# Two empty steps in the chain that scales an attention block by its softmax sums, and another split of the row-max tiles between two stages

## The chip, the cores and the metric

The kernel runs on one core of a Trainium2 chip. The metric is device time in microseconds (us), measured over whole executions; lower is better. Beside the times there is one profiled execution, whose trace tells what each engine did: TensorE (PE, with its weight loads as PEld), VectorE (DVE), ScalarE (ACT), GpSimd (POOL) and SyncE (SP), which here only issues DMAs. Every engine takes its instructions in the order in which the program wrote them.

## The reference

One input x of 2048 tokens by 640 channels goes through two branches that a gate mixes:

```python
g = sigmoid((x * gate_w).sum(-1, keepdims=True))
# a: attention, 32 query heads of 20 channels, one shared key and value head
q = (x @ wq), k = x @ wk, v = x @ wv
p = softmax(q k^T * 20 ** -0.5);  a = (p @ v) @ wo
# b: token-mixing MLP, along the tokens: 2048 -> 1728 -> 2048
h = layernorm(x);  u = gelu(h^T w1 + b1);  b = (u w2 + b2)^T
out = g * a + (1 - g) * b
```

All data are 32-bit floats. Products that need it are made from a high and a low part of each operand (three matmuls for one).

## The kernel before, in words

**Attention.** A unit n (0 to 31) is one block of 512 queries for a group of four heads; it has sixteen key blocks of 128 keys. For each key block PE makes four score tiles (L703, operands K=62 rows, in two row halves of the array), ScalarE takes their exponentials (L712), and `pv_group` (L728) multiplies them with v for all four heads into one bank (sixteen L738 matmuls for two key blocks). A column of ones behind v gives the softmax sums in the same bank, one row for each head. ScalarE copies the bank out (L747, L750) and POOL adds the copies up in `acc` (L751).

The exponent needs the maximum of each row beforehand. For that PE makes the scores of every unit a second time, as *max tiles* (L491), 32 for each row half and unit, 2048 in all, and VectorE reduces each to a column (L497). After 64 tiles VectorE takes the final maximum (L512), POOL negates and splits it (L514 to L516), and VectorE turns it (L523); the result goes through DRAM (m_scr) into two rows of the q tile (L531).

**The chain of a unit's sums.** When a unit's last key blocks are added up, `pv_group` puts a list of steps into `later`. In the loop these are: `sums_out` (L773, four rows of sums to l_scr in DRAM), `sums_in` (L776, back as 128x16 into `rl`), `inverse` (L780, VectorE's reciprocal, and its DMA to l_scr, L781), `inverse_in` (L785, four broadcast reloads into `ot`), `scale` (L789, POOL multiplies acc by ot), `high` (L792, POOL) and `low` (L795, POOL, and eight stores to o_scr, L799). The output product reads o_scr. In the tail (`keep`) the chain is another one, all on VectorE and POOL.

**Stretches.** `main(k, ...)` (L1096) writes one stretch of the order: score tiles, max tiles and 15 to 24 steps of another product, dealt to the two row halves by a pattern of letters and a small model of when PSUM banks come free, and at its end the PV group of two key blocks. There are 244 stretches (`ph`): 84 with the first MLP product (L1004), 128 with the second (L816), 32 with the output product of the first eight row tiles (L949). A unit lasts eight of them. `settle()` (L1060) is called in the middle of a stretch and at its end; each call takes one step from `later` (two once all max tiles are done, `spare`) and one from the gelu chain. So a chain of seven steps lasts three and a half stretches. At the end of a stretch the order is: `ms_done` (the final maximum), `settle`, `fetch_max`, the `rest` of the stretch (loads and splits of weights on SP and POOL, L105 to L130), `store_max`, and then the PV group.

**Shares of max tiles.** `share(k)` (L1079) says how many max tiles each half gets in stretch k. `base` holds what the pattern has. Up to `m` (the end of the first MLP product) a stretch gets its pattern, less one in every fourth; from `m` on, the tiles that are left are dealt in proportion to the patterns that are left:

```python
        if k >= m:
            return [(x * c[k] + sum(c[k:]) // 2) // sum(c[k:]) for x, c in zip(left, base)]
```

**Tail.** After the stretches come 13 blocks with the last 26 key blocks, the output products of the other row tiles (L904, added up by VectorE, L912) and late loads from o_scr (L879); before them the program asserts that `later` is empty.

Of the kernel before, what the change touches and what calls it, by code (L numbers as in the profile page):

```python
# [32 lines left out]
NA = 8  # L33
# [7 lines left out]
def mix_kernel(ctx: ExitStack, tc: tile.TileContext, A_x, A_wq, A_wk, A_wv, A_wo,  # L41
# [5 lines left out]
    def f32(ap):  # L47
        return ap.bitcast(F32)
# [123 lines left out]
    with tc.tile_pool(name="pa", bufs=1) as pa, \  # L172
# [114 lines left out]
        def transpose_x(sb, cs):  # L287
            pts = [(pst if c < 4 else psa).tile([P, NB], F32, name="pt" if c < 4 else "pp") for c in cs]
            for i in range(4):
                for c, pt in zip(cs, pts):  # L290
                    nc.tensor.transpose(pt[:, i * P:(i + 1) * P], xts[4 * sb + i][:, c * P:(c + 1) * P], ident)
            return [(sb, c, pt) for c, pt in zip(cs, pts)]
# [102 lines left out]
        for sb in range(NQB):  # L395
# [11 lines left out]
            for m in range(DC):  # L407
                turned = []
                if sb + 1 < NQB and m > 1 and (sb, m) != (2, DC - 1):
                    turned = transpose_x(sb + 1, ((0, 1), (2, 3), (4,))[m - 2])  # L410
# [46 lines left out]
    def bank_take():  # L457
        i = min(range(len(pool)), key=lambda j: pool[j][0])
        return pool.pop(i)[1]
# [8 lines left out]
    def busy(engine, us):  # L468
        clock[engine] = max(clock[engine], clock["now"]) + us
# [256 lines left out]
    later = []  # L726

    def pv_group(us, keep=False):  # L728
        n, kb = units[us[0]]
        assert units[us[-1]][0] == n  # L730
        if not otile:
            otile.append(bank_take())
        o = otile[0]
        opened = not keep or kb == 0 or us[0] == len(units) - TAIL
        ends = kb + len(us) == NS
        for i, u in enumerate(us):
            for hh in range(4):
                nc.tensor.matmul(o[32 * hh:32 * hh + 32, :], v_sb[:, kb + i, :], ptiles.pop((u, hh)),  # L738
                                 start=opened and i == 0, stop=(i == len(us) - 1) and (ends or not keep),
                                 skip_group_check=True)  # L740
        if not keep:
            begin = max(clock["act"], clock["pv"] + 0.14)
            clock["act"] = begin + 0.477
            pool.append((begin + 0.65, otile.pop()))
            if kb == 0:
                sums[0] = ev.tile([P, NB], F32, name="acc", bufs=2)
                nc.scalar.activation(sums[0], o, AF.Copy)  # L747
            else:
                part = ev.tile([P, NB], F32, name="part", bufs=2)
                nc.scalar.activation(part, o, AF.Copy)  # L750
                nc.gpsimd.tensor_add(sums[0], sums[0], part)  # L751
        if ends and n < NU - 1:
            qb, g = divmod(n, NQ)
            ot = ev.tile([P, NB // 32, 32], F32, name="ot")
            rl = ev.tile([P, NB // 32], F32, name="rl")
            on = sums[0]
            flat = ot.rearrange("p c e -> p (c e)")
            oh, ol = flat.bitcast(F32R), on.bitcast(F32R)
            if keep:
                nc.vector.tensor_add(on, on, o)  # L760

            def turned():
                nc.vector.transpose(flat, on)
                nc.vector.reciprocal(rl, ot[:, :, DH])
                nc.vector.tensor_mul(ot, ot, rl[:, :, None].to_broadcast([P, NB // 32, 32]))

            def back():
                nc.vector.transpose(on, flat)

            def sums_out():  # L770
                for hh in range(4):
                    r = 32 * hh + DH
                    nc.sync.dma_start(out=l_scr[0, n, hh:hh + 1], in_=on[r:r + 1, :])  # L773

            def sums_in():
                nc.sync.dma_start(out=rl, in_=l_scr[0, n].rearrange("h (r c) -> (h r) c", r=32))  # L776

            def inverse():
                busy("dve", 0.17)
                nc.vector.reciprocal(rl, rl)  # L780
                nc.sync.dma_start(out=l_scr[1, n].rearrange("h (r c) -> (h r) c", r=32), in_=rl)  # L781

            def inverse_in():
                for hh in range(4):
                    nc.sync.dma_start(out=flat[32 * hh:32 * hh + 32, :],  # L785
                                      in_=l_scr[1, n, hh:hh + 1].to_broadcast([32, NB]))

            def scale():
                nc.gpsimd.tensor_mul(on, on, flat)  # L789

            def high():
                nc.gpsimd.tensor_copy(oh, on)  # L792

            def low():
                nc.gpsimd.tensor_sub(ol, on, f32(oh))  # L795
                for j, t in enumerate((oh, ol)):
                    for hh in range(4):
                        r = (4 * g + hh) * DH
                        nc.sync.dma_start(out=o_scr[j, r:r + DH, qb * NB:(qb + 1) * NB],  # L799
                                          in_=f32(t[32 * hh:32 * hh + DH, :]))  # L800

            first = (None, turned, back) if keep else (sums_out, sums_in, inverse, inverse_in, scale)
            later.extend((False, f) for f in (*first, high, low))

    def b2_jobs(st):
# [226 lines left out]
    def stretches(seq):  # L1032
        return [(rows[1 - b], rest if b else [], done if b else []) for rows, rest, done in seq for b in range(2)]

    ph = stretches(seq)
    m = len(ph)
# [37 lines left out]
    def pattern(k):  # L1074
        return PATTERN[len(ph[k][0]) if visits[k] else 0]

    base = [[pattern(k)[int(k % 2 != h)].count("m") for k in range(len(ph))] for h in range(2)]

    def share(k):  # L1079
        left = [32 * NU - x for x in given]  # L1080
        if k >= m:
            return [(x * c[k] + sum(c[k:]) // 2) // sum(c[k:]) for x, c in zip(left, base)]
        over = [sum(c[k:]) - x for x, c in zip(left, base)]
        h = over.index(max(over))
        return [c[k] - (i == h and k % 4 == 1 and over[h] > 0) for i, c in enumerate(base)]

    lanes = [0.0, 0.0]
    fresh = [True, True]
# [7 lines left out]
    def main(k, vs, n_max):  # L1096
# [65 lines left out]
        if vs:  # L1162
            start = max([max(lanes) + DRAIN, min(e for e, _ in pool)] + [ready[v] for v in vs])
            clock["pv"] = start + len(vs) * PV_US + ENTER
            lanes[:] = [clock["pv"]] * 2
            fresh[:] = [True, True]
            pv_group(vs)
# [7 lines left out]
    for k in range(len(ph)):  # L1175
        n = visits[k]
        main(k, list(range(v, v + n)), share(k))
        v += n
        if k == len(ph) - 4:
            raw = last_wo()  # L1180
        if k == len(ph) - 2:
            w_last = split_last(raw)
# [4 lines left out]

    pool.append((lanes[0], ps_g.tile([P, NB], F32, name="g")))
    begin = lanes[0]
    assert not later  # L1190
    otile.append(bank_take())
    for i in range(4):
        tail_load(NS - 4 - NA + i, late=True)
# [1 line left out]
    for n in BLOCKS:  # L1195
# [25 lines left out]
        for _ in range(n):  # L1221
            settle()
            pv_group([v], True)
            v += 1
# [88 lines left out]
```

## Time and profile before

| | us |
|---|---|
| median of 3 runs | 1626.67 |
| lowest and highest | 1624.76, 1627.72 |
| the profiled execution's own time | 1627.24 |
| its span in the trace | 1625.4 |

The granted TensorE clock was 1.00 throughout. In the rows of the profile, `out<-in` names tiles, x the count; a number behind `<-` is idle time of the engine just before the instruction, and what ended it. Rows of the chain that ended last are: start, duration, engine, tile and line.

### The profile page before, as it was taken

The page shows a single profiled execution, that of the slowest core. Times are in us where ns is not written, and L with a number is a line of the kernel's source. Part 1 is how long each engine was busy: PE and PEld are TensorE (multiplying, and loading weights), DVE is VectorE, ACT ScalarE, POOL GpSimd, SP SyncE. Part 2 cuts the span into 40 slices and gives each one's busy share as a digit, 9 for nine tenths or more (in the row PEclk, how much of TensorE's full clock was granted, in tenths as well). Part 3 has the DMA queues.
Part 4 walks back from the last instruction along what each step waited for, and adds up shares of the span by engine and source line. Part 5 has one row for each costly group of instructions (what it writes and reads, how often), then busy time and mean ns, then how long its engine had stood idle before and what let it go on. Part 6 is the DMA issues. An engine that isn't in the chain of part 4 may idle for free.

```text
span 1625.4 us, 39511 instructions
## 1 busy us (share of the span) xinstructions
PE 1616.6 (99%) x14877; PEld 1127.4 (69%) x14877; DVE 1351.8 (83%) x2344; ACT 1311.0 (81%) x2567; POOL 866.6 (53%) x974
## 2 busy tenths in 40 slices
PE   9999999999999999999999999999999999999999
PEld 7899677677777777666666666666666666666666
DVE  6689999999999999888888888888888888667623
ACT  4445888788888888888888888888888888999975
POOL 6568676886777677644544344344444433333410
PEclk9999999999999999999999999999999999999999
DMA  7755222323332232222222121222222212245521
GB/s 211 213 161 149 72 74 73 89 76 82 84 84 79 73 78 67 64 72 81 72 71 72 57 74 55 66 66 80 73 72 72 68 53 64 88 111 188 149 76 44
DMA packets 188244, 144.50 MB, mean 89 GB/s; under 512 B 43473, under 2 KB 150126, under 8 KB 188054
## 3 DMA queue, kind: packets, MB, share of 16 engines
q1 hardware_dynamic: 187766, 141.66, 31.2%
q8 instruction: 117, 1.92, 0.5%
q14 instruction: 73, 0.60, 0.1%
q10 hardware_dynamic: 288, 0.33, 0.1%
HBM read 108.38 MB, written 32.15 MB: 86 GB/s over the span
## 4 chain that ended last, share of the span: by engine, by line
PE 97%; DMA 1%; SPq 1%; DVE 1%; ACT 0%; POOL 0%; issue 0%; DVEq 0%; ACTq 0%; POOLq 0%
PE ms L738 18%; PE g L816 11%; PE ms L703 9%; PE g L1004 9%; PE s L703 9%; PE s L738 8%; PE s L491 7%; PE ms L491 5%; PE pp L299 4%; PE pu L624 3%; PE o L703 3%; PE o L738 2%; PE o L491 2%; PE g L949 2%; PE ml L491 1%; PE ms L904 1%
## 5 line engine op out<-in xcount | busy, mean ns | idle before, releaser
L497 DVE TENSOR_REDUCE mp<-s 128x1 f32<-128x512 f32 x910 | 595.0, 679 | 91.1 <-PE s L491 76.8
L712 ACT ACTIVATE p<-ms 128x512 f32<-128x512 f32 x940 | 542.4, 616 | 47.5 <-PE s L738 17.5
L497 DVE TENSOR_REDUCE mp<-ms 128x1 f32<-128x512 f32 x748 | 493.6, 679 | 58.7 <-PE ms L491 45.5
L712 ACT ACTIVATE p<-s 128x512 f32<-128x512 f32 x813 | 474.7, 612 | 36.4 <-PE ms L738 10.6
L751 POOL TENSOR_TENSOR acc<-acc,part 128x512 f32<-128x512 f32 x212 | 273.8, 1292 | 392.3 <-ACT part L750 380.2
L491 PE MATMUL s<-kst,qmx 60*128 60x512 f32 x910 | 366.1, 417 | 0.6 <-DVE yo L547 0.5
L703 PE MATMUL ms<-qst,kst 62*128 62x512 f32 x940 | 359.7, 408 | 0.3 <-ACT part L750 0.2
L703 PE MATMUL s<-qst,kst 62*128 62x512 f32 x813 | 325.1, 412 | 0.4 <-ACT p L712 0.2
L1004 PE MATMUL g<-slot,wh 64*128 64x320 f32 x1344 | 306.4, 312 | 0.0
L738 PE MATMUL ms<-p,v_sb 128*32 128x512 f32 x2544 | 305.9, 598 | 0.0
L491 PE MATMUL ms<-kst,qmx 60*128 60x512 f32 x748 | 296.3, 411 | 0.0
L1004 PEld LDWEIGHTS g<-slot,wh 64*128 64x128 f32 x1344 | 216.8, 184 | 68.7 <-issue 54.5
L130 POOL TENSOR_TENSOR wl<-wr,wh 128x512 fp32r<-128x512 f32 (+1 forms) x176 | 218.1, 1239 | 29.5 <-ACT wh L127 9.8
L497 DVE TENSOR_REDUCE mp<-o 128x1 f32<-128x512 f32 x298 | 202.4, 679 | 22.1 <-PE o L491 16.0
L1004 PE MATMUL g<-slot,wl 64*128 64x320 f32 x672 | 205.3, 305 | 0.0
L703 PEld LDWEIGHTS ms<-qst,kst 62*128 62x128 f32 x940 | 171.8, 185 | 48.2 <-ACT p L712 24.7
L703 PEld LDWEIGHTS s<-qst,kst 62*128 62x128 f32 x813 | 150.1, 185 | 72.6 <-ACT p L712 41.6
L816 PE MATMUL g<-slot,wh 64*128 64x320 f32 x864 | 197.4, 310 | 0.0
L816 PE MATMUL g<-u,wh 64*128 64x320 f32 x864 | 196.7, 309 | 0.6 <-POOL wh L129 0.6
L712 ACT ACTIVATE p<-o 128x512 f32<-128x512 f32 x280 | 172.2, 615 | 12.5 <-PE ms L738 5.3
L491 PEld LDWEIGHTS s<-kst,qmx 60*128 60x128 f32 x910 | 166.3, 185 | 7.3 <-DVE mp L497 1.7
L738 PEld LDWEIGHTS ms<-p,v_sb 128*32 128x32 f32 x2544 | 66.4, 109 | 135.1 <-issue 95.2
(247 smaller groups left out, 3159.6 us busy)
## 6 DMA issues: line engine op xcount, KB each, us to landing
wr<-in_B_w_dram SPq DMA_DIRECT2D x136, 256.0 KB
qmx<-q_scr SPq DMA_DIRECT2D x192, 80.0 KB
qst<-q_scr SPq DMA_DIRECT2D x192, 80.0 KB
ot<-l_scr SPq DMA_DIRECT2D x120, 64.0 KB
y_scr<-yo SPq DMA_DIRECT2D x16, 320.0 KB
slot<-o_scr SPq DMA_DIRECT2D x16, 320.0 KB
o_scr<-ot SPq DMA_DIRECT2D x124, 40.0 KB
o_scr<-acc SPq DMA_DIRECT2D x124, 40.0 KB
```

The source lines that it names most:

```text
L130: nc.gpsimd.tensor_sub(wl[:, :nv], wr[:, :nv], f32(wh[:, :nv]))
L299: nc.tensor.matmul(pp, w, t, start=first and n == 0, stop=not more and n == len(steps) - 1)
L491: nc.tensor.matmul(ms, qmax[n][64 * b:64 * b + 60, pr, qt * P:(qt + 1) * P], kst[64 * b:64 * b + 60, kq * NB:(kq + 1) * NB], start=True, s ...
L497: r = nc.vector.tensor_reduce(mtiles[n][:, c, kq:kq + 1], ms, axis=AX.X, op=ALU.max)
L624: nc.tensor.matmul(pu[r][:, :HD2], w[rows, c, :], h[rows, st, :], start=(st == 0 and k == 0), stop=(st == NS - 1 and k == 2))
L703: nc.tensor.matmul(s, kst[64 * b:64 * b + 62, kb * P:(kb + 1) * P], q[64 * b:64 * b + 62, pr, :], start=True, stop=True)
L712: e = nc.scalar.activation(p, s, AF.Exp, scale=SCALE)
L738: nc.tensor.matmul(o[32 * hh:32 * hh + 32, :], v_sb[:, kb + i, :], ptiles.pop((u, hh)), start=opened and i == 0, stop=(i == len(us) - 1) a ...
L751: nc.gpsimd.tensor_add(sums[0], sums[0], part)
L816: other_tile(half, nc.tensor.matmul(hold["p"][:, :HD2], w[r, i, :], u[d][r, fc, :], start=(hold["n"] == 1), stop=(hold["n"] == 6 * FC - 3)))
L949: other_tile(half, nc.tensor.matmul(hold["p"][:, :HD2], o[r, c, :], w[r, c, d * HD2:(d + 1) * HD2], start=(hold["n"] == 1), stop=(hold["n" ...
L1004: other_tile(half, nc.tensor.matmul(hold["p"][:, :HD2], w[r, st % HS, :], h[d][r, st, :], start=(hold["n"] == 1), stop=(hold["n"] == 6 * NS)))
```

## The change

Three edits. The chain of a unit's sums gets two steps that do nothing: one between `sums_in` and `inverse`, one between `inverse_in` and `scale`; it has nine steps then and lasts four and a half stretches. `share` deals the exact counts of the patterns up to the end of the second MLP product (244 - 32 = 212 stretches) and in proportion only in the last 32; the one tile less in every fourth stretch stays with the first product. And where the program asserted that `later` is empty at the end of the stretches, it now runs what is left of it.

```diff
-            first = (None, turned, back) if keep else (sums_out, sums_in, inverse, inverse_in, scale)
+            first = (None, turned, back) if keep else (sums_out, sums_in, None, inverse, inverse_in, None, scale)
             later.extend((False, f) for f in (*first, high, low))
...
     def share(k):
         left = [32 * NU - x for x in given]
-        if k >= m:
+        if k >= len(ph) - 4 * NA:
             return [(x * c[k] + sum(c[k:]) // 2) // sum(c[k:]) for x, c in zip(left, base)]
         over = [sum(c[k:]) - x for x, c in zip(left, base)]
         h = over.index(max(over))
-        return [c[k] - (i == h and k % 4 == 1 and over[h] > 0) for i, c in enumerate(base)]
+        return [c[k] - (i == h and k % 4 == 1 and k < m and over[h] > 0) for i, c in enumerate(base)]
...
     pool.append((lanes[0], ps_g.tile([P, NB], F32, name="g")))
     begin = lanes[0]
-    assert not later
+    while later:
+        f = later.pop(0)[1]
+        if f:
+            f()
     otile.append(bank_take())
```

## The prediction

> **What bounds the kernel now.** I read the page first, then the chain that ended last, then the waits, and last the timelines of single engines at the places that the chain names. A stretch is the time from one start of a PV group (sixteen L738 matmuls) to the next; The stretches of scores, max tiles and MLP or output products fill most of the span; the 13 blocks of the tail come behind them.
>
> ```profile
> PE 1616.6 (99%) x14877; PEld 1127.4 (69%) x14877; DVE 1351.8 (83%) x2344; ACT 1311.0 (81%) x2567; POOL 866.6 (53%) x974
> ```
>
> TensorE leads, but 99% doesn't mean that 1% is left: two row halves are fed by one queue in order, and when its head waits, the other half's pipelined matmuls still count as busy. Lost time is seen in the length of a stretch. The chain gives the starts:
>
> ```profile
> 218.14 1.85 PE ms L738 x16
> 224.20 1.85 PE ms L738 x16
> 230.16 1.85 PE ms L738 x16
> ...
> 289.80 1.85 PE ms L738 x16
> 296.42 1.92 PE ms L738 x16
> ...
> 660.65 1.85 PE ms L738 x16
> 667.25 1.85 PE s L738 x16
> ...
> 697.16 4.46 DMA rl<-l_scr
> 701.82 2.43 DVE mp L497 x4
> ...
> 713.00 1.85 PE ms L738 x16
> ...
> 757.74 1.85 PE s L738 x16
> ```
>
> In the first MLP product a stretch takes 5.96 us (224.20 to 230.16). From there on PE sets its own pace, and there are a few exceptions: 6.06 (218.14 to 224.20), 6.62 (289.80 to 296.42), 6.60 (660.65 to 667.25). In the second product eight stretches take 44.74 us (713.00 to 757.74, 5.59 each), but the eight before, 667.25 to 713.00, took 45.75, and inside them the chain leaves PE for a reload `rl<-l_scr` and for VectorE. So what the change can win are the exceptions; the pace itself it leaves alone.
>
> ```profile
> POOL acc L789 <- DMA qst<-m_scr: 62.0, 17, 6.1
> ...
> DVE rl L780 <- DMA rl<-l_scr: 6.5, 8, 1.4
> ```
>
> These two waits are the ones into which the empty steps go. L789 (`scale`) reads only acc and ot, so the DMA it waits for is the reload of ot, whatever name the row carries. POOL's waits cost something only where PE ends up behind them.
>
> **The change part by part.** *The first empty step (ahead of `inverse`).* It moves the reciprocal L780 by half a stretch, from the middle of the second stretch of a chain to its end. The reciprocal's own DMA into l_scr moves with it on SP, behind the loads of q in that stretch. On VectorE it now comes behind the second half of the stretch's max tiles instead of in front of them:
>
> ```profile
> 701.65 0.25 DVE L780 RECIPROCAL rl<-rl 128x16 f32<-128x16 f32 x1 [1.40 <-DMA rl<-l_scr]
> ```
>
> VectorE stood 1.40 us and four max tiles stood behind it (2.43 us), so their PSUM banks came back late. PE lost 45.75 - 44.74 = 1.01 us, 0.72 of the wait. At the new place VectorE arrives four tiles, about 2.4 us, later; the longest wait in the row is 1.4, so all eight should go. Price: the seven in the stretches of the second product have 6.5 - 0.92 (the eighth, below) = 5.6 us; at 0.72 that is 4.0, at nothing for the shorter ones (a wait of a few tenths can be caught up by VectorE, which is 83% busy) about 2.8. I take **3.4**.
>
> The eighth lies in the second to last stretch of the output products:
>
> ```profile
> 1528.40 1.92 PE L738 MATMUL o<-p,v_sb 128*32 128x512 f32 x16
> 1534.48 1.92 PE L738 MATMUL s<-p,v_sb 128*32 128x512 f32 x16 [0.88 <-DVE mp L497]
> ```
>
> ```profile
> 1533.63 0.25 DVE L780 RECIPROCAL rl<-rl 128x16 f32<-128x16 f32 x1 [0.92 <-DMA rl<-l_scr]
> ```
>
> 6.08 us, where a stretch with the same number of tiles takes 5.09 (row 1453.69, below): **1.0**.
>
> Where nothing waits, the reciprocal itself still costs in the first product:
>
> ```profile
> 222.86 0.24 DVE L780 RECIPROCAL rl<-rl 128x16 f32<-128x16 f32 x1
> ...
> 226.53 0.69 DVE L497 TENSOR_REDUCE mp<-s 128x1 f32<-128x512 f32 x1 [0.50 <-PE s L491]
> ```
>
> It stands ahead of the last tiles of its stretch, and the stretch that holds it (218.14 to 224.20, as PE counts it) is the 6.06 one, 0.10 over its neighbour. At the end of the stretch it falls into the 0.50 us in which VectorE waits for PE anyway, and 0.24 fits. Ten chains (units 0 to 9) lie in this product: 10 x 0.10 = **1.0**. If the cover is gone (another small reduction, L512 or L523, at the same end) it costs at most the 0.10 again.
>
> *A rule against this step.* The Trainium skill, "DMA: Bandwidth & Descriptors", section "Anatomy of one DMA", puts the fixed cost of one DMA at about 2.0 us, for the path through GpSimd. By that an 8 KB reload issued at 697.16 would be there before VectorE comes to it, the step would win nothing in the second product, and the sum would lack the 3.4. The row has 4.46 us on SP's queue, and VectorE waiting at its end; the trace disagrees, and I go by the row.
>
> *The second empty step (ahead of `scale`).* With the first, `scale`, `high` and `low` come one whole stretch later on POOL and the eight o_scr stores one stretch later on SP; `inverse_in` half a stretch later. POOL is in order, and behind `scale` stood the split of MLP weights:
>
> ```profile
> 664.15 1.29 POOL L789 TENSOR_TENSOR acc<-acc,ot 128x512 f32<-128x512 f32 x1 [5.14 <-DMA qst<-m_scr]
> 665.50 0.61 POOL L792 CAST ot<-acc 128x512 fp32r<-128x512 f32 x1
> 666.05 0.51 POOL L129 CAST wh<-wr 128x384 fp32r<-128x384 f32 x1
> ```
>
> ```profile
> 666.61 0.41 PE L816 MATMUL g<-u,wh 64*128 64x320 f32 x1 [0.58 <-POOL wh L129]
> ```
>
> PE waits for that wh: 6.60 against 5.59, **1.0**. After the change the split (issued at the end of that stretch) is ahead of `scale` in POOL's order and goes as soon as POOL is free, so this is gone whatever `scale` then waits. The other place is unit 1:
>
> ```profile
> 282.64 1.29 POOL L789 TENSOR_TENSOR acc<-acc,ot 128x512 f32<-128x512 f32 x1 [5.92 <-DMA m_scr<-mt]
> ```
>
> ```profile
> 292.47 0.47 ACT L552 ACTIVATE yo<-yo 128x320 f32<-128x320 f32 x1 [1.84 <-POOL yo L562]
> ```
>
> POOL's backlog reaches a gelu product, ScalarE waits 1.84 for it, and the exps behind it hold PE: 6.62 - 5.96 = **0.7**. At the new place POOL comes one stretch (5.96 or 5.6) later and the data at most half a stretch (3.0) later, so a wait of 5.92 shrinks to 3 or less and the usual ones to about nothing. I take the whole 0.7; nothing of it is the other end. The remaining POOL waits (most of the 62) hold up nobody now, so their end is worth nothing. The later stores cost nothing either: by the order of the program the loads that read o_scr come stretches after them, except those of the last unit.
>
> *The last unit (29).* Now the chain no longer ends inside the loop; `high` and `low` are flushed behind it (third edit). On POOL this puts the row maxima's split (L514 to L516) ahead of `scale`. Before, it was behind:
>
> ```profile
> 1546.83 0.21 DVE L523 STREAM_TRANSPOSE mt<-mn 128x32 f32<-128x32 f32 x1 [6.00 <-POOL mn L516]
> ```
>
> ```profile
> PEld o L703 <- DVE yo L912: 0.7, 1, 0.7
> ```
>
> VectorE stood 6.00 us for that split, the tail's first additions (L912) stood behind it, and a weight load of PE waited 0.7 for a bank. The load runs ahead of the matmul a little, so I count **0.5** of it (between none and 0.7). Against it, `high` and `low` come behind one more 1.29 us addition, so the late loads of the tail are some 1.3 us later; the tail first finishes four whole row tiles that are loaded already, so that is covered. Without the cover it would be 1.3.
>
> *Max tiles.* I worked the counts out of `share` and the patterns. When the second product begins, 598 and 599 tiles of the two halves are left, and the patterns from there on hold 592 each, 512 of them in the product: 13 extra tiles. The proportional rule puts 2 of them into the product (stretches 207 and 210) and 11 into the output products; the new one puts all 13 into the latter, at 223 and 226 for the two.
>
> ```profile
> 1353.03 1.92 PE L738 MATMUL s<-p,v_sb 128*32 128x512 f32 x16
> 1359.09 1.92 PE L738 MATMUL s<-p,v_sb 128*32 128x512 f32 x16
> ```
>
> ```profile
> 1448.90 1.92 PE L738 MATMUL ms<-p,v_sb 128*32 128x512 f32 x16
> 1453.69 1.92 PE L738 MATMUL ms<-p,v_sb 128*32 128x512 f32 x16
> 1458.78 1.92 PE L738 MATMUL s<-p,v_sb 128*32 128x512 f32 x16
> ```
>
> With nine tiles a stretch of the product takes 6.06 against 5.59, some of it for one more MLP step in such a stretch, so 0.4; an extra tile in the output products makes 5.09 of 4.79, 0.3. Net 2 x (0.4 - 0.3) = **0.2**.
>
> Sum: 3.4 + 1.0 + 1.0 + 1.0 + 0.7 + 0.5 + 0.2 = 7.8 us. The profiled execution took 1627.24 (span 1625.4), 0.6 over the median of the runs, 1626.67; from the median, 1626.67 - 7.8 = **1618.9 us**. What is late next is PE's own pace.
>
> **The rivals.** *The wait moves along.* The reload of rl, or the way of the reciprocal through SP and DRAM, is held up by what SP has queued (q loads), so VectorE waits at the end of the stretch instead. The row against it: the longest wait is 1.4 and the step gives 2.4. Then the 3.4 and 1.0 are lost and the 1.0 of the first product with them: 1626.67 - 2.4 = 1624.3, no change that can be told (I count 0.2%, 3.3 us, as that bound). Chance 0.1.
>
> *POOL pays at the new place (slower).* The write of the reciprocal is now issued behind up to twelve q loads; if ot lands so much later that `scale` still waits, it stands ahead of other work: gelu products, sums, output rows. It decides from a wait of about 5 us, since 5.14 and 5.92 cost PE 1.0 and 0.7. If it did so in all chains, ten at 0.7 and twenty at 1.0 would be 27 us against the 5.9 that stay (3.4, 1.0, 1.0, 0.5): 1626.67 + 27 - 5.9 = 1648. Against it: the splits of weights are ahead of `scale` now, and POOL is 53% busy. Chance 0.04.
>
> *It does nothing for PE.* If the exceptions were PE's own pace in another form and the waits only stood beside them, only the 0.2 would come: 1626.5. Against it speaks that the chain itself goes through rl at 697.16. Chance 0.04.
>
> **How the numbers follow.** My case has 0.82; its own range is 1616.5 to 1622 (2.8 to 4.0 for the waits, the small ones in or out). Rivals of no change have 0.14 together, the slower one 0.04. The range 1616 to 1623.2 holds my case and some of what lies between it and the first rival. Faster by over 0.2% 0.84, within 0.2% 0.11, slower 0.05.
>
> **What would show it.** Right: no row of L780 waiting for rl in the waits; the 62.0 of `scale` down to below 25; the 6.06 stretches of the first product gone and no 6.6 among them; thirteen stretches of 5.09 in the output products; L523's wait of 6.00 down to about 1. Wrong: L780 waiting at ends of stretches, stretches that are long one later than before (POOL at its new place), or a later start of the tail's last matmuls though the loop ends earlier.

## The result, and the profile after

| | us |
|---|---|
| kernel before, median of 6 runs | 1627.03 (1624.76 to 1627.73) |
| changed kernel, median of 6 runs | 1620.58 (1620.21 to 1621.32) |
| ratio of the two, 95% interval | 0.9962 [0.9949, 0.9975] |
| profiled execution before, after | 1627.24, 1621.32 |
| its span before, after | 1625.4, 1619.5 |

The change makes the kernel 6.4 us faster by the medians and 5.9 us by the spans. The forecast was 1618.9, 7.8 less than before. It holds in sign and nearly in size; what is missing is found below, stretch by stretch. The busy times of the page, line for line against those of before:

```profile
PE 1612.7 (100%) x14877; PEld 1126.8 (70%) x14877; DVE 1352.9 (84%) x2344; ACT 1309.9 (81%) x2567; POOL 867.9 (54%) x974
```

Nothing here tells what happened: the same work, 5.9 us less time around it. The chain that ended last tells more. In its first line, the shares by engine, the DMA, SPq and POOL of before (2% together in rounded shares) are gone:

```profile
PE 99%; DVE 1%; ACT 0%; issue 0%; DVEq 0%; ACTq 0%
```

Pieces of the chain at the three places of the prediction (start, us, what):

```profile
289.78 1.85 PE ms L738 x16
...
295.73 1.85 PE ms L738 x16
...
665.12 1.85 PE s L738 x16
...
709.89 1.85 PE ms L738 x16
...
726.63 1.91 PE ms L738 x16
...
732.37 1.85 PE o L738 x16
```

289.78 to 295.73 is the stretch that the prediction read as 6.62 (6.67 by the starts of the PV groups themselves; the chain cuts some rows by 0.07): it takes 5.95 now, PE's own pace. 665.12 to 709.89 are the eight stretches that took 45.75: 44.77, against 44.74 for eight without a wait. The last pair, 726.63 to 732.37, is a stretch that takes 5.68 us by PE's timeline (726.61 to 732.29), and that is new: before, the stretches of this kind took 5.57 to 5.59. More on it below.

The waits. L780 has no row any more; `scale` (L789) waited 101 us in all in its four rows of before, and now has these:

```profile
POOL acc L789 <- DMA ot<-l_scr: 20.0, 15, 3.0
...
POOL acc L789 <- DMA qst<-m_scr: 5.3, 1, 5.3
```

With a third row of 0.8 us that is 26. The timeline of VectorE shows where the reciprocal stands now, in the first product and in the stretch that had the chain's wait of 1.40:

```profile
224.81 1.28 DVE L497 TENSOR_REDUCE mp<-s 128x1 f32<-128x512 f32 x2
226.01 0.24 DVE L780 RECIPROCAL rl<-rl 128x16 f32<-128x16 f32 x1
226.58 0.69 DVE L497 TENSOR_REDUCE mp<-s 128x1 f32<-128x512 f32 x1 [0.33 <-PE s L491]
```

```profile
700.44 0.24 DVE L780 RECIPROCAL rl<-rl 128x16 f32<-128x16 f32 x1
700.60 0.15 DVE L523 STREAM_TRANSPOSE mt<-mn 128x32 f32<-128x32 f32 x1
701.10 1.29 DVE L497 TENSOR_REDUCE mp<-s 128x1 f32<-128x512 f32 x2 [0.35 <-PE s L491]
```

In both, the next max tile behind the reciprocal still waits for PE (0.33 and 0.35 us): VectorE comes to its work before PE has made it, even where L523 falls to the same end. So the cover named in the prediction was there, and the 0.24 us of the reciprocal hold up nobody.

In the last unit, the split of the row maxima is ahead of `scale` on POOL, and VectorE's wait for it fell from 6.00 to 1.67 us. These are POOL's timeline and then VectorE's:

```profile
1537.02 0.23 POOL L516 TENSOR_TENSOR mn<-mm,mn 128x16 fp32r<-128x16 f32 x1
1540.27 1.29 POOL L789 TENSOR_TENSOR acc<-acc,ot 128x512 f32<-128x512 f32 x1 [3.02 <-DMA ot<-l_scr]
```

```profile
1537.28 0.21 DVE L523 STREAM_TRANSPOSE mt<-mn 128x32 f32<-128x32 f32 x1 [1.67 <-POOL mn L516]
```

POOL still waits 3.02 us for ot, and no row of PE waits for it. PE's PV groups there:

```profile
1524.12 1.92 PE L738 MATMUL o<-p,v_sb 128*32 128x512 f32 x16
1529.25 1.92 PE L738 MATMUL ms<-p,v_sb 128*32 128x512 f32 x16
...
1539.78 1.92 PE L738 MATMUL s<-p,v_sb 128*32 128x512 f32 x16
...
1545.22 1.92 PE L738 MATMUL s<-p,v_sb 128*32 128x512 f32 x16
```

1524.12 to 1529.25 is the stretch in which VectorE waited 0.92 us for rl: 5.12 where it took 6.08. 1539.78 to 1545.22 is the first one of the tail: 5.44 where it took 6.17.

The other signs that the prediction named came nearly all: thirteen stretches of the output products take 5.07 to 5.12 (eleven before), no stretch of the first product takes 6.6, and nine of its ten stretches of 6.06 are gone. Three came short. L523's wait fell to 1.67 us, not to about 1. Its "62.0 of `scale`" was one row of four that make 101, and of these 26 are left, not below 25. And not every wait of `scale` shrank to 3 us: the one of 5.3 stands in the output products, in a stretch of 4.78 us that loses nothing by it.

### The profile page after: what moved, and what is told of

Its sections match the earlier page's. It is cut to its first block, busy times and chain, and to the rows that moved or that the text cites. A ratio compares the mean times of both kernels' runs of the same rounds, so it can differ in the third digit from the quotient of the medians.

```text
span 1619.5 us, 39566 instructions
## 1 busy us (share of the span) xinstructions
PE 1612.7 (100%) x14877; PEld 1126.8 (70%) x14877; DVE 1352.9 (84%) x2344; ACT 1309.9 (81%) x2567; POOL 867.9 (54%) x974
## 3 DMA queue, kind: packets, MB, share of 16 engines
q8 instruction: 117, 1.92, 0.5%
## 4 chain that ended last, share of the span: by engine, by line
PE 99%; DVE 1%; ACT 0%; issue 0%; DVEq 0%; ACTq 0%
PE ms L738 16%; PE g L816 11%; PE s L738 10%; PE ms L703 10%; PE g L1004 9%; PE s L703 8%; PE s L491 7%; PE ms L491 6%; PE pp L299 4%; PE pu L624 3%; PE o L703 3%; PE o L738 3%; PE o L491 2%; PE g L949 2%; PE ml L491 1%; PE ms L904 1%
## 5 line engine op out<-in xcount | busy, mean ns | idle before, releaser
L497 DVE TENSOR_REDUCE mp<-s 128x1 f32<-128x512 f32 x895 | 586.4, 680 | 68.1 <-PE s L491 56.7
L497 DVE TENSOR_REDUCE mp<-ms 128x1 f32<-128x512 f32 x763 | 503.3, 680 | 69.5 <-PE ms L491 58.6
L712 ACT ACTIVATE p<-s 128x512 f32<-128x512 f32 x818 | 480.2, 616 | 33.2 <-PE ms L738 10.7
L703 PE MATMUL ms<-qst,kst 62*128 62x512 f32 x938 | 366.5, 409 | 0.1
L491 PE MATMUL s<-kst,qmx 60*128 60x512 f32 x895 | 358.6, 415 | 0.6 <-DVE yo L547 0.5
L703 PE MATMUL s<-qst,kst 62*128 62x512 f32 x818 | 322.4, 409 | 0.2 <-ACT p L712 0.2
L491 PE MATMUL ms<-kst,qmx 60*128 60x512 f32 x763 | 302.4, 411 | 0.0
L738 PE MATMUL ms<-p,v_sb 128*32 128x512 f32 x2272 | 273.2, 598 | 0.0
L703 PEld LDWEIGHTS ms<-qst,kst 62*128 62x128 f32 x938 | 171.5, 185 | 61.5 <-ACT p L712 29.0
L703 PEld LDWEIGHTS s<-qst,kst 62*128 62x128 f32 x818 | 151.2, 185 | 53.7 <-ACT p L712 35.6
L738 PE MATMUL s<-p,v_sb 128*32 128x512 f32 x1424 | 171.2, 598 | 0.2 <-ACT p L712 0.2
```

What stands on the lines that cost most here:

```text
L491: nc.tensor.matmul(ms, qmax[n][64 * b:64 * b + 60, pr, qt * P:(qt + 1) * P], kst[64 * b:64 * b + 60, kq * NB:(kq + 1) * NB], start=True, s ...
L497: r = nc.vector.tensor_reduce(mtiles[n][:, c, kq:kq + 1], ms, axis=AX.X, op=ALU.max)
L703: nc.tensor.matmul(s, kst[64 * b:64 * b + 62, kb * P:(kb + 1) * P], q[64 * b:64 * b + 62, pr, :], start=True, stop=True)
L712: e = nc.scalar.activation(p, s, AF.Exp, scale=SCALE)
```

## The experiments

Eight runs were made, of seven kernels, in two groups; each was compared with the kernel before on its own chip (1626.77 us there for 1, 2, 4 and 6, and 1624.67 for 3, 5, 7 and 8).

**1. The first empty step alone.** The share of max tiles is the old one, as in 2 and 3; the third edit, which runs what is left of the chain, is in all of them.

```diff
-            first = ... (sums_out, sums_in, inverse, inverse_in, scale)
+            first = ... (sums_out, sums_in, None, inverse, inverse_in, scale)
```

> Only the empty step between sums_in and inverse; max tiles shared as before; what is left of the chain is run behind the stretches. Theory: the reload of rl has half a stretch more, so no row of L780 waits for rl (gain 3.5 in the second product, 1.0 near the end), the reciprocal leaves the ten 6.06 stretches (1.0), and the row maxima's split comes ahead of scale at the end (0.7); reload and scale move together, so POOL's wait at L789 stays near 100 us in all and the 6.6 stretches near 290 and 660 us stay or shift. Against it 14 stretches of the second product are 0.10 longer for two more semaphore instructions at the first score of a unit (1.5). Sum 6.2 - 1.5 = 4.7 faster than before. Rival (the gain comes from POOL's order, the second step): less than 2 faster.

Measured: 1646.62 us (1645.78 to 1649.24), ratio 1.0124 [1.011, 1.0138]. Half of the change is 20 us *slower* than nothing. What it was to win it did win: no row of L780, the 6.06 stretches of the first product gone but for one. But `scale` waits 158 us in all, in five rows; the longest of them:

```profile
POOL acc L789 <- DMA ot<-l_scr: 117.3, 21, 8.2
...
PEld g L816 <- POOL wh L129: 19.6, 16, 3.2
```

The second row says who pays: PE's weight loads for the second product, which read wh. One such place, POOL's timeline, PE's matmul behind it, and PE's PV groups around it:

```profile
1041.28 1.26 POOL L789 TENSOR_TENSOR acc<-acc,ot 128x512 f32<-128x512 f32 x1 [7.65 <-DMA ot<-l_scr]
1042.48 0.50 POOL L129 CAST wh<-wr 128x384 fp32r<-128x384 f32 x1
```

```profile
1043.04 0.41 PE L816 MATMUL g<-u,wh 64*128 64x320 f32 x1 [2.40 <-POOL wh L129]
```

```profile
1035.18 1.92 PE L738 MATMUL o<-p,v_sb 128*32 128x512 f32 x16
1043.62 2.98 PE L738 MATMUL s<-p,v_sb 128*32 128x512 f32 x16
1050.67 1.92 PE L738 MATMUL ms<-p,v_sb 128*32 128x512 f32 x16
```

8.44 and 7.05 us in place of 5.58 each. With one empty step, `inverse` goes out half a stretch later and `scale` comes half a stretch later, so its data has no more lead than before; and `scale` has moved from the middle of a stretch to the end, where the split of weights that is issued in that stretch's `rest` stands right behind it. In the sixteen stretches of the second product that have `scale` in them, 21.2 us were lost against before, and another 4.0 in three stretches right behind such ones. The second PV group above shows what these three are: its matmuls take 2.98 us for 1.92. PE's busy time and granted clock around it:

```profile
1043.00:1044.30 1.30, 1.26 (x10) 1.00 0.00 0
1044.40:1047.70 3.30, 3.30 (x19) 0.50 0.20 60
1047.80:1050.60 2.80, 2.80 (x32) 1.00 0.27 64
```

The third last column is the clock: about 3.4 us at half of it, just behind PE's wait of 2.40. There are three such periods in this execution, from 668.9, 812.3 and 1044.4 on, and none in the loops of the kernel before and of the changed one. At half the clock about half of each is lost, by that estimate 5 us of the 22 by which the two spans differ, the 4.0 among them. So long waits were paid for twice here, the greater part as the wait itself; why three of the sixteen places set it off and the others did not is open.

This is the slower rival of the prediction, in half of the change, and in the second product its threshold held: with the split right behind it, each of the sixteen waits of 5.2 to 8.2 us cost PE between 0.5 and 3.0 us. The expectation had the sign wrong, because it let `scale` keep its place among the weights.

**2. The second empty step alone.**

```diff
-            first = ... (sums_out, sums_in, inverse, inverse_in, scale)
+            first = ... (sums_out, sums_in, inverse, inverse_in, None, scale)
```

> Only the empty step between inverse_in and scale; max tiles shared as before; what is left of the chain is run behind the stretches. Theory: L780 still waits for rl (6.5 us or so) and the ten 6.06 stretches stay; scale comes half a stretch later for data that land as before, so POOL's wait at L789 falls from 101 to below 40 us, the 6.67 and 6.60 stretches fall to 5.96 and 6.0 (0.7 + 0.6), the tail wins 0.7; no new semaphore instructions at the first score. Sum 2.0 faster than before. Rival (VectorE's place doesn't matter, POOL's does): 5 or more faster.

Measured: 1624.29 (1622.36 to 1626.96), ratio 0.9987 [0.9978, 0.9996]; the span of its profile was 1622.6, 2.8 less than before. The gelu stretch of unit 1 is repaired (6.67 to 5.95) and so is the end (0.75). VectorE waits for rl as before. What stood idle ahead of the two instructions, from the views of L780 and of L789:

```profile
  DMA rl<-l_scr: 7.0, 11
```

```profile
  DMA qst<-m_scr: 50.2, 15
  DMA ot<-l_scr: 30.8, 10
  DMA m_scr<-mt: 8.0, 2
```

The total is near the expected one, two details are not: POOL's wait fell only from 101 to 89 us, and the 6.60 stretch stayed (6.55, from a PV group at 659.54 to one at 666.09). POOL's timeline there, with the split of weights right behind `scale` as before:

```profile
663.73 1.28 POOL L789 TENSOR_TENSOR acc<-acc,ot 128x512 f32<-128x512 f32 x1 [5.76 <-DMA qst<-m_scr]
664.97 0.50 POOL L129 CAST wh<-wr 128x384 fp32r<-128x384 f32 x1
```

So this step alone puts `scale` at the same bad place as the first one alone, but here `inverse` goes out as early as before, and the waits are shorter: in the second product all but this one are 2.4 to 4.2 us, and the stretches that hold them stay at 5.56 or 5.57. Alone, the two steps are worth +20 and -2.5 us; together they are worth about -6. They don't add: each alone puts `scale` at the end of a stretch, both together put it back in the middle, one stretch later, with its data there.

**3. `scale` of experiment 1 behind the split.** This undoes only POOL's order: the chain of experiment 1, but where `scale` falls to the end of a stretch it is issued behind `rest`, so behind that stretch's split.

```diff
-                if f:
+                if f and wide and not spare[0] and f.__name__ == "scale":
+                    behind_rest.append(f)
+                elif f:
                     f()
...
-        for f in rest:
+        for f in rest + behind_rest:
             f()
+        behind_rest.clear()
```

> As the kernel with the first empty step alone, but where scale falls on the end of a stretch it is issued behind the splits of MLP weights of that stretch instead of ahead of them; nothing else moves. Theory: that kernel lost 20 us because scale, waiting 5 to 8 us for ot, stood on POOL ahead of the split of weights that PE needs in the next stretch; with the split ahead of it the long stretches (6.1 to 9.4) go back to 5.57, and it is 4 to 5 us faster than the kernel before, though scale waits as long. Rival (the later write of the reciprocal and what it does to SP's queue and its loads cost the 20 us): still more than 10 slower than before.

Measured: 1620.68 (1620.24 to 1621.43), ratio 0.9975 [0.9965, 0.9985]. All of the 20 us are gone and 4.0 are won. `scale` still waits long:

```profile
POOL acc L789 <- DMA ot<-l_scr: 66.0, 25, 5.6
```

and at one such place, POOL's timeline and PE's:

```profile
1017.60 1.28 POOL L130 TENSOR_TENSOR wl<-wr,wh 128x512 fp32r<-128x512 f32 x1
1020.82 1.30 POOL L789 TENSOR_TENSOR acc<-acc,ot 128x512 f32<-128x512 f32 x1 [1.94 <-DMA ot<-l_scr]
```

```profile
1016.98 1.92 PE L738 MATMUL o<-p,v_sb 128*32 128x512 f32 x16
1022.54 1.92 PE L738 MATMUL s<-p,v_sb 128*32 128x512 f32 x16
```

5.56 us, PE's own pace, with POOL waiting in the middle of it. The waits are shorter too (73 us in all for 158), because POOL now does the splits in that time, and ot is there sooner: at this place 3.84 us behind the PV group, 6.10 in experiment 1. But the edit moves nothing except `scale` on POOL, and the granted clock stays at 1.00. So the cause of the 20 us is shown: the split of weights behind a long wait of `scale` on POOL.

**4. The place of the reciprocal alone.** The changed kernel with a second reciprocal, of a column that is there from the start, in the old place. Its result is read by nobody and it waits for no DMA.

```diff
-... (sums_out, sums_in, None, inverse, inverse_in, None, scale)
+... (sums_out, sums_in, lambda: nc.vector.reciprocal(ev.tile([P, NS], F32, name="idle"), g_col), inverse, ...
```

> As the changed kernel, but in place of the first empty step, in the middle of the stretch, VectorE makes a reciprocal of a constant column that nobody reads and that waits for nothing. Theory: the place alone costs 0.10 in the first product, so the ten stretches (units 0 to 9) go from 5.95 back to 6.06 and nothing waits for rl; in the second product nothing changes. 1.0 slower than the changed kernel. Rival (the 0.10 came from a wait on the reload): the stretches stay at 5.95.

Measured: one run, 1621.17, without the changed kernel beside it on that chip, so the total can't tell 1 us. The stretches can: nine stretches of the first product went back from 5.95 to 6.06 (1.0 us in all), the second product did not change. PE's timeline:

```profile
217.41 1.92 PE L738 MATMUL ms<-p,v_sb 128*32 128x512 f32 x16
223.47 1.92 PE L738 MATMUL ms<-p,v_sb 128*32 128x512 f32 x16
229.43 1.92 PE L738 MATMUL ms<-p,v_sb 128*32 128x512 f32 x16
```

6.06, then 5.96: a VectorE instruction of 0.24 us in the middle of a stretch costs PE 0.10 there without any wait, as the prediction's third term had it. In the second product the place costs nothing by itself, so what was won there hangs on the wait for rl.

**5. The empty step ahead of the reload.** As many steps as in the changed kernel, and every step from `inverse` on at the same place; only the reload `sums_in` is half a stretch later, so its lead over the reciprocal is the old one.

```diff
-            first = ... (sums_out, sums_in, None, inverse, inverse_in, None, scale)
+            first = ... (sums_out, None, sums_in, inverse, inverse_in, None, scale)
```

> As the changed kernel, but the first empty step stands ahead of sums_in instead of between sums_in and inverse: every step from inverse on is where the changed kernel has it, only the reload of rl is half a stretch later and behind one more stretch end's loads on SP. Theory (what counts is the lead of the reload over the reciprocal): L780 waits for rl again, in most units, 1 to 2 us each, and 3 to 8 us of the gain are lost. Rival (what counts is that the reciprocal comes behind the max tiles of its stretch): no loss, within 0.5 us of the changed kernel.

Measured: 1644.46 (1638.02 to 1645.61), ratio 1.0123 [1.0107, 1.0138]. The place is the new one, the lead the old one, and the result is 24 us worse than the changed kernel. VectorE waits again, and more than it did before the change:

```profile
DVE rl L780 <- DMA rl<-l_scr: 23.2, 14, 7.0
```

The direction was foreseen, the size (3 to 8 us) not. The loss of the profiled execution (span 1636.2) lies mostly in four stretches of the output products, 7.50, 7.01, 11.51 and 7.88 us for 4.79 to 5.08; only about 1.9 us lie in the two MLP products. In the second of them VectorE's short waits for rl, up to 0.32 us, cost nothing at this place; two longer ones, 0.57 and 1.70, cost 0.2 and 1.3. The longest of the four, on VectorE and on PE:

```profile
1502.38 0.25 DVE L780 RECIPROCAL rl<-rl 128x16 f32<-128x16 f32 x1 [7.00 <-DMA rl<-l_scr]
```

```profile
1494.67 1.92 PE L738 MATMUL s<-p,v_sb 128*32 128x512 f32 x16
1506.18 2.77 PE L738 MATMUL ms<-p,v_sb 128*32 128x512 f32 x16
```

Here the reload was issued on SP at 1499.22, 9.4 us after the sums had gone out (1489.78), behind the loads of the next unit's q. The expectation priced it like the old waits of about a microsecond and left SP's queue out. The PV group at the end of that wait takes 2.77 us for 1.92: here too the granted clock fell,

```profile
1501.20:1507.90 6.70, 4.58 (x24) 0.50 0.18 47
1548.90:1552.30 3.40, 3.40 (x21) 0.50 0.38 129
```

and what PE does in that time takes twice as long. The other timed runs of this kernel lie 6.1 to 7.6 us above its profiled execution, and their granted clock is 0.994 or 0.995 where that has 0.996. Over 1640 us that can be 1.6 to 3.3 us of the gap; the rest is not explained.

**6. The reciprocal's write in four parts.** This tests the new stretches of 5.7 us. In the second product the last stretch of a unit grew from between 5.57 and 5.59 to between 5.67 and 5.73 in fourteen units, 1.6 us in all. The order on PE is the same there, and no wait is longer. What differs is in the view of line L703 (the score tiles): instructions of PE's sequencer that only wait for a semaphore, count and ns, before and then after:

```profile
L703 PEldq EVENT_SEMAPHORE  x103: 51/51/51, 161.7 to 1565.8; - x103
```

```profile
L703 PEldq EVENT_SEMAPHORE  x144: 51/51/51, 161.9 to 1559.8; - x144
```

41 more, 51 ns each. Ahead of the first score of a new q tile there are five in place of three, 0.10 us. The tile is filled by ten DMAs (six loads of q, four reloads of row maxima, L531), and SP's DMAs are counted on eight semaphores in turn (the trace keeps their numbers, 101 and 103 to 109, though no view prints them). Before, the four reloads of `inverse_in` stood between the loads and the row maxima; after the change only the single write of the reciprocal does. So the ten DMAs fall on seven different semaphores in the units of the second product, six before, and need more waits. If that is the cause, three more DMAs in the write's place, four again between the two groups, should undo it. The edit is in the changed kernel:

```diff
-                nc.sync.dma_start(out=l_scr[1, n].rearrange("h (r c) -> (h r) c", r=32), in_=rl)
+                for h in (slice(0, 32), slice(32, 64), slice(64, 96), slice(96, P)): nc.sync.dma_start(out=l_scr[1, n].rearrange("h (r c) -> (h r) c", r=32)[h], in_=rl[h])
```

> As the changed kernel, but the reciprocal's write to l_scr goes out as four DMAs of 32 partitions. Theory: what PE waits for at the first score of a unit are ten DMAs of its q tile (six loads, four of the row maxima), counted on eight semaphores in turn. With one DMA between the loads and the row maxima they fall on more different semaphores (five semaphore instructions ahead of the matmuls instead of three), with four between them they share them as before: three again, the 14 stretches of 5.68 go back to 5.58, 1.5 us faster than the changed kernel, about 1619 where that has 1620.6. Rival (the 0.10 is a wait for data of the q tile, or comes from VectorE): 5.68 stays, time within 0.3 us of the changed kernel or above it.

Measured: 1619.49 (1619.11 to 1619.72), ratio 0.9954 [0.9941, 0.9968]. The ten DMAs fall on six semaphores again, and these stretches are back at 5.57 or 5.58 (with that of a fifteenth unit, which took 5.70 before the change too), 1.7 us in all.

**7 and 8. The changed kernel and this version on one chip.** The same two kernels as above, side by side.

> The changed kernel, unchanged, on the same chip as the others of this call: 1620.6, 6 us below the kernel before.

> The changed kernel with the reciprocal's write in four DMAs, again, beside the changed kernel on one chip. Theory: fourteen stretches 0.10 to 0.14 shorter, 1.3 to 1.7 us below the changed kernel. Rival: the two are within 0.5 us.

Measured: the changed kernel 1620.07 (1619.90 to 1620.24), ratio 0.9971 [0.9959, 0.9982]; with the write in four 1618.62 (1618.44 to 1618.98), ratio 0.9961 [0.9949, 0.9974]. The runs of the two don't overlap: 1.45 us less. The row of the semaphores and the stretch that took 5.68, on PE's timeline:

```profile
L703 PEldq EVENT_SEMAPHORE  x101: 51/51/51, 161.0 to 1557.0; - x101
```

```profile
725.64 1.92 PE L738 MATMUL ms<-p,v_sb 128*32 128x512 f32 x16
731.22 1.92 PE L738 MATMUL o<-p,v_sb 128*32 128x512 f32 x16
```

5.58 us. So four small DMAs beat one here, and this version beats both kernels. It is not free: in both of its profiles one stretch of unit 23 grew from 5.57 to 5.85. And beside the changed kernel on this chip, experiment 3 (1620.68, without the new share of max tiles) lies only 0.6 us higher: the right place on POOL is worth nearly as much as the second empty step.

## Why the prediction was right, and where it was off

| term of the sum | predicted | measured, by stretches |
|---|---|---|
| waits for rl in the second product | 3.4 | 3.5 |
| the last unit's wait | 1.0 | 0.96 |
| the reciprocal in the first product | 1.0 | 0.97 |
| POOL, the 6.60 stretch | 1.0 | 0.61 |
| POOL, the gelu stretch | 0.7 | 0.72 |
| the tail | 0.5 | 0.73 |
| max tiles | 0.2 | 0.2 |
| semaphores on PE | not in the sum | -1.6 |
| sum | 7.8 | 6.1 |

The column on the right compares the length of each stretch in the two profiles. Its sum is 0.2 above the difference of the spans; the rest lies in small changes elsewhere.

- *The waits for rl* were sized between 2.8 (the long ones alone) and 4.0 (0.72 of each), and 3.5 lies there: the mechanism and the size were right. Seven stretches of 5.72 to 6.58 came back to 5.57 or 5.58. That nothing was to be won without the wait is shown by experiment 4 (the place costs nothing in the second product); that the longer lead ended it, by experiment 5 (the old lead at the new place brings the waits back). The new place helped too: with the old lead it lost only 1.5 us in the second product, not 3.5. The rule of the Trainium skill that was weighed against this term ("DMA: Bandwidth & Descriptors", section "Anatomy of one DMA") would have made it nothing; the row of 4.46 us disagreed, and 3.5 us were won.
- *The first product*: nine of ten stretches went from 6.06 to 5.95; that of unit 9 went only to 6.03. The stretch ahead of that one, which holds no reciprocal, takes 6.03 or 6.04 in both kernels too, so something else is late there, and what was not looked into.
- *POOL, the 6.60 stretch*: the mechanism was right, the size was not. It takes 5.99 now, 0.4 over PE's pace. The weight load of its last max tile waits 0.23 us for a bank that VectorE frees; where the rest of the 0.4 goes was not looked into. The step that failed is taking a stretch's whole excess for one wait.
- *POOL, the gelu stretch*: 0.72 by the starts of the PV groups (6.67 to 5.95). The prediction had 0.66 from two rows of the chain that are cut differently and rounded it to 0.7.
- *The tail*: 0.73, the upper end of the bound (0.7), not its middle.
- *Max tiles*: the two stretches with nine tiles fell from 6.06 and 6.09 to 5.66, two others grew from 4.79 to 5.09 and 5.12.
- *The term that is missing*: "The reciprocal's own DMA into l_scr moves with it on SP, behind the loads of q in that stretch." and "`inverse_in` half a stretch later" counted where these DMAs stand in SP's queue, and stopped there. That their order also decides how many semaphores PE has to look at ahead of a q tile is 1.6 us, most of the gap between the forecast and the result. Experiments 6 to 8 and the semaphore numbers in the traces show that the number of DMAs between the two groups decides it.
- *The slower rival* had 0.04 and did not come; but experiment 1 shows that it is real and stands half a stretch away from the change. The argument against it ("the splits of weights are ahead of `scale` now") was the one that decides, not POOL's 53%: POOL was 53% busy in experiment 1 too.
- *It does nothing for PE* and *the wait moves along* are ruled out by the 44.77 us for eight stretches and by the missing row of L780.

Not tried: the new share of max tiles by itself, which is read from the traces only.

## What to carry to other kernels

Moving a step changes two things at once, the lead between a transfer and its use and the step's neighbours on its in-order engine. Read both: here the first empty step alone had the better neighbours on VectorE and the worse ones on POOL, and was 20 us slower until its neighbours on POOL were put right. A wait of an idle engine has no price of its own; its price is what stands behind it, so look for the first instruction behind it whose result the bounding engine reads.

## What the hardware showed that was not expected

- One DMA in place of four between two groups of loads made the kernel slower: 41 more semaphore instructions of 51 ns on PE's sequencer, 0.10 to 0.15 us for a stretch, though PE's matmuls, their order and their waits for data were the same. Here the wait for ten DMAs was paid on PE: three instructions when the ten fell on six semaphores, five when they fell on seven.
- Waits of PE can cost more than their own length: in experiments 1 and 5 the granted clock fell to 0.50 for 3.4 us (6.8 us at one place) during or just behind some of PE's waits, where the kernel before and the changed one have 1.00.
- PE's busy share rose from 99% to 100% while it did the same work in 5.9 us less; neither figure shows the lost time, the starts of the PV groups do.
